# Full-height score matmuls, merged output blocks and a six-slot pipeline in an attention and mixture-of-experts kernel

## The chip, the cores and the metric

The kernel runs on one core of a Trainium2 chip. The metric is the device time of one execution in microseconds (us). "Span" is the time from the first to the last instruction in the trace of one profiled execution.

With one core, a run's state (fast or slow) is known only from its time against the fastest run of the same kernel. Ratios are the mean time of one kernel's fast runs over that of the other's fast runs of the same rounds, so they are not quite the ratio of the medians quoted beside them. A ratio comes with its 95% interval.

In lines of the profile, PE is TensorE's matmuls, PEld its weight loads, DVE VectorE, ACT ScalarE, POOL GpSimd, and L288 is line 288 of the kernel. Brackets hold the idle time before an instruction and what ended it. PSUM is the memory that the matmuls of these kernels write to; copying a result out of it is called evacuating.

## The reference

```python
def attention(q, k, v):              # (4, 8, 768, 64)
    scores = (q @ k.T) / 8
    # heads 0, 2, 6: causal; the other five: causal and (key < 4 or distance < 64)
    a = softmax(masked scores)
    return a @ v

def moe(x, w_skip, w_gate, w1, w2):  # x: (3072, 512), the heads side by side
    todo = (x @ w_skip) > 0          # about half of the tokens
    e = argmax(x @ w_gate); g = softmax(x @ w_gate)[e]       # 8 experts
    out = x
    out[todo] += g * (relu(x @ w1[e]) @ w2[e])               # 512 -> 1024 -> 512
```

Nothing of the second half can start for an expert until every batch has been routed, because a token's place in its expert's list depends on all tokens before it.

## The kernel before

Attention works batch by batch in three passes. `trans` turns Q and K of two heads at a time so that the 64 features lie on the rows of the array. `retr` (causal heads) and `strm` (windowed heads) compute transposed scores, the exponential on ScalarE and a mask. `avx` forms one block of 128 output rows of the batch before, normalizes it, writes it out, casts it, transposes it and computes the gates.

```python
    def trans(b, pr):
        for name, src, dst in (("qT", q_in[b], qT), ("kT", k_in[b], kT)):
            ps = tp.tile([P, NT, P], FP16, tag="t", name="tps")
            for n in range(NT):
                for i, h in enumerate(PAIRS[pr]):          # two heads, 64 rows each
                    nc.tensor.matmul(ps[i * D:(i + 1) * D, n],
                                     src[:, h, n * D:(n + 1) * D], ident, is_transpose=True, ...)
            # ... evacuated alternately by ScalarE and VectorE

    def retr(b, pr, i, c):
        r = slice(i * D, (i + 1) * D)
        # ...
        nc.tensor.matmul(ps[:, o:o + w], kT[b, pr][r, j * P:(j + 1) * P],
                         qT[b, pr][r, q0:q0 + w], start=True, stop=True)

    def avx(b, i):
        for t in range(2):
            o = ap_.tile([P, 4, V1], FP32, tag=f"av{t}", name=f"av{t}")
            # ... output matmuls of four heads, then reciprocal and multiply on VectorE
        # ... DMA of the block
        nc.gpsimd.tensor_copy(x16, xf)                     # cast on GpSimd
        for s in range(DS):
            nc.tensor.matmul(ps[:, s], x16[:, s * P:(s + 1) * P], ident, is_transpose=True, ...)
        nc.scalar.copy(xT, ps)
        # ... gates, at once

    for b in range(B + 1):
        steps = list(front(b)) if b < B else []
        if b < B:
            prep_v(b)                  # copies of V on GpSimd, at the start of the batch
        for i in range(NT):
            if b:
                avx(b - 1, i)
            for f in steps[i * len(steps) // NT:(i + 1) * len(steps) // NT]:
                f()
        if b:
            route(b - 1)
        if b + 2 < B:
            load_qk(b + 2, False)
            load_v(b + 2)
        if b + 1 < NW and b < B:       # NW = 5 experts are loaded in attention
            load_w(b + 1)
```

The experts follow. Sixteen indirect DMAs gather the tokens of eight experts by 128-row tiles, the loads of the other three experts' weights are mixed in among them, and then come two matmul passes and a scatter for each expert.

```python
        for e in range(3):
            gather(e)
        load_w(NW)                     # takes the buffer of the first expert
        for e in range(3, E):
            gather(e)
        for e in range(NW + 1, E):
            load_w(e)
```

The softmax here doesn't subtract the row's maximum and nothing guards it: scores larger than these inputs give would overflow.

## Time and profile before

| | us |
|---|---|
| time, median of the runs beside the changed kernel | 287.84 (286.45 to 289.05) |
| the profiled execution: time, span | 276.55, 274.6 |
| to the last block's gates (attention) | 188.5 |
| from there to the first expert matmul | 14.2 |
| experts | 61.6 |
| end | 10.3 |

The profiled execution was some 10 us faster than every timed one.

One more page row is worth reading. The row of the granted clock (the share of TensorE's full speed, in tenths), in 40 slices of the span:

```profile
PEclk9999999999999999955555555555559999999995
```

It shows nines (full speed) up to about 117 us. The first record of the clock lies at 106.1 us, where a fast stretch of 10.2 us begins. Ahead of this record the row showed full speed while score matmuls of 512 columns took 604 ns (40 to 60 us), against 387 in the fast stretch, so for that part only durations tell. The prediction shows them, with the stages and the waits.

### The profile page before, as it was taken

Reading aid. Unit: us, or ns where it says so; the run is one execution under the profiler, and the core shown is the slowest. Engines: PE = TensorE matmul, PEld = TensorE weight load, DVE = VectorE, ACT = ScalarE, POOL = GpSimd, SP = SyncE. Lnnn points to the kernel's source line nnn. Section 1 sums busy time; section 2 is a strip of 40 time slices with the busy share of each in tenths; the row PEclk is TensorE's granted clock in tenths of the full one; section 3 lists DMA queues with packets and bytes.
Section 4 is the critical chain, followed back from the end, with each engine's and each line's share of the span. In section 5 each row is a group of like instructions: output and inputs, shape, how many; then the busy total and the mean of one; then the engine's idle time right before and its main releaser. Section 6 shows DMA issues by size and latency. Waiting matters only on the chain. (4 is left out here: it accounts for less than half of the span.)

```text
span 274.6 us, 5032 instructions
## 1 busy us (share of the span) xinstructions
PE 207.7 (76%) x1996; PEld 130.6 (48%) x1996; DVE 120.9 (44%) x398; ACT 96.2 (35%) x138; POOL 121.4 (44%) x182
## 2 busy tenths in 40 slices
PE   1797038999838059999599999992179999999940
PEld 0454014655524046665355665661147666666620
DVE  5337104434418125657744357546334454554330
ACT  2568101273822007774055464121033323232200
POOL 8869399525123364281610110110477718325240
PEclk9999999999999999955555555555559999999995
DMA  5997999999999999999020010220276999998110
GB/s 70 164 114 72 191 175 223 247 216 225 227 209 180 216 154 195 235 207 105 24 84 11 38 41 35 83 79 38 66 204 193 160 262 218 211 260 217 42 62 7
DMA packets 53457, 39.52 MB, mean 144 GB/s; under 512 B 28265, under 2 KB 44649, under 8 KB 53424
## 3 DMA queue, kind: packets, MB, share of 16 engines
q0 software_dynamic: 49968, 32.82, 80.2%
q10 hardware_dynamic: 1728, 3.15, 3.2%
q1 hardware_dynamic: 1728, 3.15, 3.2%
q8 instruction: 17, 0.28, 0.4%
q14 instruction: 16, 0.13, 0.2%
HBM read 56.66 MB, written 10.49 MB: 245 GB/s over the span
## 5 line engine op out<-in xcount | busy, mean ns | idle before, releaser
L295 ACT ACTIVATE atr<-sps 128x1024 f16<-128x1024 f32 (+1 forms) x36 | 32.4, 919 | 14.8 <-PE sps L288 14.5
L382 POOL CAST x<-x 128x512 f16<-128x512 f32 x24 | 15.0, 629 | 45.4 <-DVE x L377 26.3
L388 ACT COPY xT<-tps 128x512 f16<-128x512 f16 x24 | 14.1, 587 | 56.4 <-PE tps L385 46.0
L574 PE MATMUL mhp<-mxT,w1t 128*128 128x256 f16 x256 | 30.4, 279 | 0.9
L376 DVE RECIPROCAL rec<-av 128x4 f32<-128x4 f32 x48 | 8.6, 181 | 49.9 <-PE av L366 34.0
L589 PE MATMUL myp<-w2t,ht 128*128 128x512 f16 x128 | 29.9, 379 | 0.0
L366 PE MATMUL av<-va,atr 128*128 128x65 f16 x252 | 23.4, 236 | 7.5 <-POOL va L242 7.5
L574 PEld LDWEIGHTS <-w1t 128*128 128x128 f16 x256 | 25.7, 100 | 7.0 <-issue 2.8
L288 PE MATMUL sps<-qT,kT 64*128 64x512 f16 (+3 forms) x96 | 28.6, 450 | 0.1
L593 POOL DMA_INDIRECT out_dram<-xg,idx x16 | 16.2, 1011 | 26.4 <-DVE xg L591 9.3
L385 PE MATMUL tps<-ident,x 128*128 128x128 f16 x96 | 14.4, 295 | 16.5 <-POOL x L382 16.5
L107 POOL DMA_DIRECT2D va<-in_v_dram x24 | 21.2, 948 | 11.4 <-DMA w2t<-in_moe_w_dram 5.3
L366 PEld LDWEIGHTS <-atr 128*128 128x128 f16 x252 | 15.0, 120 | 15.5 <-issue 13.5
L542 POOL DMA_INDIRECT xg<-out_dram,idg x16 | 16.5, 1030 | 12.8 <-DVE idx L529 8.2
L265 DVE COPY qT<-tps 128x768 f16<-128x768 f16 x16 | 15.3, 958 | 14.6 <-PE tps L255 13.1
L578 DVE TENSOR_SCALAR ht<-mhp 128x512 f16<-128x512 f32 x16 | 11.1, 691 | 23.9 <-PE mhp L574 23.9
L371 PE MATMUL av<-vs,ats 128*64 128x65 f16 x120 | 18.6, 247 | 3.7 <-POOL vs L248 2.0
L377 DVE TENSOR_TENSOR x<-av,rec 128x256 f32<-128x256 f32 x48 | 20.1, 422 | 2.2 <-POOL x L382 0.4
L357 PE MATMUL av<-vsk,esk 20*128 20x260 f16 x48 | 18.1, 383 | 2.3 <-ACT esk L348 1.2
L567 ACT COPY mxT<-mtp 128x512 f16<-128x512 f16 x16 | 8.7, 588 | 31.6 <-PE mtp L565 21.3
L255 PE MATMUL tps<-ident,qin 128*64 128x128 f16 x192 | 14.0, 302 | 6.9 <-DMA qin<-in_q_dram 6.5
L263 ACT COPY kT<-tps 128x768 f16<-128x768 f16 x16 | 12.8, 800 | 18.0 <-PE tps L255 18.0
(130 smaller groups left out, 375.8 us busy)
## 6 DMA issues: line engine op xcount, KB each, us to landing
w1t<-in_moe_w_dram POOLq DMA_DIRECT2D x8, 1024.0 KB, 14.1
w2t<-in_moe_w_dram POOLq DMA_DIRECT2D x8, 1024.0 KB, 17.7
va<-in_v_dram POOLq DMA_DIRECT2D x24, 128.0 KB, 10.3
out_dram<-x ACTq DMA_DIRECT2D x12, 256.0 KB, 4.7
out_dram<-x SPq DMA_DIRECT2D x12, 256.0 KB, 3.7
qin<-in_q_dram POOLq DMA_DIRECT2D x3, 768.0 KB, 15.3
kin<-in_k_dram POOLq DMA_DIRECT2D x3, 768.0 KB, 14.2
qin<-in_q_dram POOLq DMA_DIRECT2D x4, 96.0 KB, 3.8
```

The source lines that it names most:

```text
L107: nc.gpsimd.dma_start(out=va[b][:, i, :, :D], in_=vr[b, i])
L265: nc.vector.tensor_copy(o, i_)
L288: mms = [lambda j=j, q0=q0, o=o, w=w: nc.tensor.matmul(ps[:, o:o + w], kT[b, pr][r, j * P:(j + 1) * P], qT[b, pr][r, q0:q0 + w], start=Tru ...
L295: nc.scalar.activation(a[:, o:o + w], ps[:, :w], ACT.Exp, scale=SCALE)
L357: nc.tensor.matmul(o, esk[b % 2][:, i * P:(i + 1) * P], vsk[:, b, t], start=True, stop=False)
L366: nc.tensor.matmul(o[:, c], a[:, x0:x0 + P], va[b][:, j, h], start=False, stop=fin and j == i)
L371: nc.tensor.matmul(o[:D, c], a[:, q0:q0 + D], vs[b][:, i, u], start=False, stop=fin)
L377: nc.vector.tensor_tensor(x[:, :, t], o[:, :, :D], rec.unsqueeze(2).to_broadcast([P, 4, D]), op=ALU.mult)
L542: nc.gpsimd.indirect_dma_start(out=xg[e, t], out_offset=None, in_=out[:, :], in_offset=bass.IndirectOffsetOnAxis(ap=idg[:, sl:sl + 1], axi ...
L574: nc.tensor.matmul(hp[:, u], w1t[:, s, f * P:(f + 1) * P], xT[:, s], start=(s == 0 and u == 0), stop=(s == DS - 1 and u == 1))
L589: nc.tensor.matmul(yp, hts[e][:, f, t * P:(t + 1) * P], w2t[:, f], start=(f == 0), stop=(f == FS - 1))
L593: sc = nc.gpsimd.indirect_dma_start(out=out[:, :], out_offset=bass.IndirectOffsetOnAxis(ap=idx[:, sl:sl + 1], axis=0), in_=xg[e, t], in_of ...
```

## The change

Its intent: let TensorE's clock be released (raised to full speed) earlier by work that uses the whole array, an idea that experiments 2 and 4 test, and let no engine wait for another inside a batch.

```diff
-NW = 5
+NW = 4
+    kz = {h: [ac.tile([P, S], FP16, name=f"kz{h}_{i}") for i in range(2)] for h in RETR}
+    # the other 64 rows of each are set to zero once, by VectorE
...
-            ps[:, o:o + w], kT[b, pr][r, j * P:(j + 1) * P],
-            qT[b, pr][r, q0:q0 + w], start=True, stop=True)
+            nc.tensor.matmul(ps[:, o:o + w], kz[h][b % 2][:, j * P:(j + 1) * P],
+                             qT[b, pr][:, q0:q0 + w], start=True, stop=True)
...
+    def fills(n):                       # ten matmuls of 512 columns before the first Q has landed
+            nc.tensor.matmul(ps[:, :512], ident, fill, start=True, stop=True)
...
-            rec = tiny.tile([P, 4], FP32, tag=f"rec{t}", name="rec")          # twice a block
+        rec = tiny.tile([P, 2, 4], FP32, tag="rec", name="rec")               # once
...
+        eng = nc.gpsimd if pool else nc.vector          # three window masks in five go to GpSimd
...
-        if b:
-            route(b - 1)                                  # in one go, at the end of a batch
+    for g in range(-NT, G + 2):                           # six slots per batch
+        for f in s0: f()                                  # scores, first half of the slot
+        gates(g - 2)
+        outp(g)
+        for f in s1: f()                                  # scores and transposes, second half
+        flush()                                           # the masks of the slot
+        xt(g - 1)
+        next(routing, None)                               # one of four pieces of the routing
...
-        for e in range(3):
+        for e in range(2):
             gather(e)
-        load_w(NW)
-        for e in range(3, E):
+        load_w(NW, wp2)                 # a pool of its own, in memory that attention gives back
+        for e in range(2, 5):
             gather(e)
-        for e in range(NW + 1, E):
-            load_w(e)
+        load_w(NW + 1, wp2)
+        for e in range(5, E):
+            gather(e)
+        for e in range(NW + 2, E):
+            load_w(e, wp2)
```

The cuts leave out that the score matmuls of two heads are no longer interleaved, fixed tiles for V whose ones and zeros are set once, V being asked for one batch later and ahead of the next Q and K, copies of V in the middle of a batch, the transposes of an expert's tokens two experts ahead, and one comparison for six in the routing.

## The prediction

> **What bounds the kernel now.** I read first the sums by stage, in the stretches that the block starts in the trace mark off: front of batch 0, output blocks of batches 0 to 3, last routing and first gathers, experts, end. The columns are the stretch, its length, then busy us (and instructions) of PE, PEld, DVE, ACT, POOL, the granted clock, the DMA share and GB/s.

> ```profile
> 0.00:35.00 35.00, 18.90 (x187) 11.19 (x188) 14.91 (x42) 16.13 (x20) 26.41 (x48) 1.00 1.25 123
> 35.00:63.20 28.20, 22.51 (x222) 13.20 (x221) 9.01 (x29) 7.96 (x11) 18.54 (x33) 1.00 1.39 216
> 63.20:116.30 53.10, 37.30 (x446) 22.86 (x445) 22.52 (x86) 22.55 (x32) 19.18 (x33) 1.00 1.31 204
> 116.30:158.10 41.80, 38.10 (x390) 22.91 (x388) 22.48 (x79) 20.03 (x29) 14.57 (x24) 0.50 0.56 80
> 158.10:188.50 30.40, 26.97 (x297) 17.35 (x295) 17.04 (x75) 11.03 (x17) 4.82 (x9) 0.50 0.16 62
> 188.50:202.70 14.20, 3.22 (x26) 2.09 (x27) 6.80 (x40) 1.50 (x4) 6.14 (x6) 0.50 0.30 84
> 202.70:264.30 61.60, 60.73 (x437) 40.98 (x436) 26.97 (x45) 17.04 (x30) 30.55 (x31) 0.98 0.86 186
> 264.30:274.60 10.30, 0.00 (x0) 0.00 (x0) 1.11 (x5) 0.00 (x0) 1.21 (x2) 0.61 0.12 38
> ```

> Attention takes 188.5 us of the 274.6, the experts 61.6 with PE busy throughout. In attention no engine but PE is busy over about half of a middle batch (41.8 us: DVE 22.5, ACT 20.0), and PE waits or runs slowly.

> Which of the two, the forms of the score matmul show. The clock column says 1.00 up to 106 us, but it has no record there; the durations decide. First the stretch 40 to 60 us, then 106.1 to 113 us.

> ```profile
> L288 PE MATMUL sps<-qT,kT 64*128 64x512 f16 x4 | 1.8, 604 | 0.0
> ...
> L288 PE MATMUL sps<-qT,kT 64*128 64x512 f16 x4 | 1.5, 387 | 0.0
> ```

> The same form takes 604 ns in one and 387 in the other. At 138 to 158 us it is 605 again. So attention runs on the slow clock from the start, apart from 106.1 to 116.3 us, and the experts (128x512 at 379 ns) on the fast one.[...]

> The third view is the waits, for the stalls; columns: total us, times, longest.

> ```profile
> PE tps L385 <- POOL x L382: 16.5, 5, 9.2
> ...
> PE av L366 <- POOL va L242: 7.5, 1, 7.5
> ...
> POOL va L107 <- DMA w2t<-in_moe_w_dram: 5.3, 1, 5.3
> ```

> PE waits 16.5 us for the cast of an output block on GpSimd. The timeline shows why: GpSimd stands in a DMA issue or behind a tile of V.

> ```profile
> 93.94 0.32 POOL L242 MEMSET va<- 128x48 f16 x1 [5.20 <-DMA va<-in_v_dram]
> ```

> Until that memset and the four copies behind it were done (98.6 us), the cast could not start, and PE stood still from 90.1 to 99.3 us. PE stands still in the same way at 27.9 to 35.4 and 74.9 to 79.7 us.

> [...]PE was busy for 3.41 of 3.41 us in several windows at the slow clock, so instruction busyness isn't what is counted. If I weigh each matmul's columns by the share of rows and columns of the array it uses, the window that released the clock (102.7 to 106.1) had 3,190 full-array columns, the greatest among the slow ones (next 2,960); the fast window before the fallback had 2,680. I take about 3,050 per window as the level: an inference from one release, not a fact. [...]six 64-row score matmuls of two heads take 1.03 us together, as three of one head do.[...]

> **The change part by part.**

> Full-height scores. Keys of heads 0, 2, 6 lie in 128-row tiles whose other half is zero. Columns per head: 1024+1024+640 = 2,688, three heads 8,064 per batch. Heads 0 and 2 no longer run side by side, nor does head 6 beside a windowed head: per batch 2,688 columns added for the first and some 2,200 for the second (three windowed heads of 768, the last beside only 640), 4,900 columns, 4.1 us slow or 2.0 us fast. In exchange these matmuls count whole: full-array columns of a batch rise from about 22,700 to 26,700 (transposes 6,144, scores 8,064, windowed 1,920, sinks 300, output 6,500, transposes of x 3,072, rest 700). Against 3,050 per 3.41 us, a batch has to last less than about 30 us to keep the clock. Before, a middle batch lasted 42.

> Fast clock. All columns of a batch that pass after one another, in the new form: transposes 6,144 (pairs side by side), scores 8,064, windowed 3,840, sinks 1,920, output 9,200, x 3,072, gates and routing about 2,900; sum 35,100.[...]

> Six slots per batch. Transposing x comes one slot after its block, gates two slots after, routing in four pieces. This takes the wait for the cast (16.5 us) off PE, and also most of PE's waits for routing. The other engines per batch: ACT nine exponentials at 0.92, five at 0.81, sinks 0.7, six copies of x at 0.59, four evacuations at 0.80: 19.8 us. DVE: nine triangle masks 2.6, two of five window masks 1.1 (three go to GpSimd), key evacuations now in six pieces, of which the half-height ones have as many columns and so also cost 0.96: 5.8, merged normalization, estimated 0.95 a block from 2 x 0.42 + 2 x 0.18 less one fixed cost, 5.7, routing about 5.5: 20.7. By slot, the larger of the engines is about 4.5 (ACT), 4.2, 5.1, 3.5 (DVE), 2.7 (PE) and 3.2 us, 23.2 in all; slot 2, say, has on DVE two triangles 0.6, a window mask 0.56, one evacuation 0.96, a normalization 0.95 and a routing piece of about 2.1. With a fifth for bubbles: 28 us a batch (estimate). It lies just under the 30 that keep the clock, so I expect the clock to flip: fast in slots 0 to 2 and 5, doubtful in 3 and 4, which have only 2,700 full-array columns (slot 3: scores 640, a windowed head 384, output 1,190, x 512).

> V and ones. The memsets inside the batches go (0.3 us each), the tiles of V are fixed, V of the next batch is asked for before its Q, K and the weights. One expert less is loaded in attention.

> Fillers. Ten matmuls of 512 columns, 4.3 us at the slow clock, in a time when PE waits for the first Q anyway (4.46 us): free, worth at most 2 to 3 us of faster transposes while DMA is the limit.

> Sum, against the stages above:
> - Front of batch 0: the loads still set it. K of batch 1 lands about 34 us, and the copies of V come after GpSimd's issues: 37 us (35.4 before).
> - Three batches with front and output: 3 x 28 = 84. The six blocks of the last batch, without other work and with one output buffer: 6 x 3.2 = 19 (before 2.4 to 4.1 us each). Two slots of drain: 4. Together 107 (153.1 before).
> - Last routing and gathers: 14.2; one comparison for six saves 1, two more gathers before the first matmul cost 1.3: 14.5.
> - Experts: 61.6, with fewer stalls but a fourth expert's weights to load here: 62.6.
> - End: 10.3.
> Sum 231.4 us of span, 43.2 less. The timed median is 13.2 us over the profiled span; I keep that: 244.6, rounded 245.

> **Rivals.** (a) The clock stays slow in most slots, because the level is higher than I think or the windows straddle slots 3 and 4. Then PE needs 29 us plus bubbles, some 34 a batch: 18 us more, 263. For it: PE was "busy" at the slow clock for nearly all of 140 to 170 us. (b) The clock stays fast throughout and slots run at engine limits: 25 a batch, 236; with the DMA-free front a little earlier, 230. For it: once fast, windows of 3,340 and 4,510 held it. (c) GpSimd becomes the wait: three window masks per batch at perhaps 1.3 us (a guess: no such row exists yet), copies of V 3.7, casts 3.8 and some ten issues of 0.9 make 20 us[...]. One slot of slack hides about 4 us; a block of 9 us per batch would cost 5 a batch, 15 in all: 260. (d) The experts wait for weights: four experts of 4.2 MB and 7 MB of gathers and scatters at the 0.43 MB per us that I estimate from the same stage before (20 MB in 47 us) need 56 us, and the last is due about 57 us in. Up to 5 us more.

> **Range and chances.** (a), (c) and (d) add, (b) takes away: 228 to 268 us holds 8 in 10. To miss 2% (282 us) nearly all of the 43 us would have to be lost, which needs (a) and (c) and a longer front: faster 0.94, within 2% 0.04, slower 0.02.

> **What would show it.** Right: 128x512 score matmuls near 385 ns in most of attention; middle batches of 25 to 30 us; no wait of a transpose of x on a cast; experts about 62 us. Wrong: 605 ns there, or records at 0.5 through whole batches (a); long GpSimd gaps ended by DMA or casts that come late (c); PE gaps before the fifth to eighth expert's matmuls that end with a weight DMA (d); a last batch of outputs well over 19 us, as the single output buffer makes every block wait for its normalization.

The stages (37 + 84 + 19 + 4 + 14.5 + 62.6 + 10.3) came to 231.4 us of span, and with 13.2 us over the span to 244.6. Cut is the step that put a batch's 35,100 columns at 29 us on the slow clock and 15 on the fast one, which rival (a) uses. The trace of the kernel before gives about the same, as an estimate: its 64-row score matmuls of 384 and 128 columns took 524 and 311 ns on the slow clock (40 to 100 us) and 323 and 216 on the fast one (106.2 to 116 us), so 0.83 and 0.42 ns per column. The 4.1 and 2.0 us for 4,900 columns agree with that.

What else the text leans on can be read in the same trace. The clock's records change at 106.08, 116.32, 205.07 and 266.51 us, 3, 26 and 18 times 3.41 us apart; these are the windows that the text weighs. An exponential took 692 ns on 20 rows and 706 on 128 for the same 640 columns, which fits the full price put on half-height evacuations (956 ns in the changed kernel, where full height had taken 958). The "fixed cost" in the merged normalization is the author's estimate; the merged multiply and reciprocal measured 692 and 207 ns, so 0.90 us against its 0.95. GpSimd spent 0.76 to 1.02 us on a DMA issue of a whole tile of V, Q, K or weights, and waited up to 5.3 us ahead of one; why it waits was not shown.

## The result, and the profile after

| | before | after |
|---|---|---|
| median, us | 287.84 | 264.6 (260.92 to 267.83) |
| ratio of the fast runs | | 0.9151 [0.9046, 0.9256] |
| profiled execution: span, us | 274.6 | 259.1 |

The output agrees with the reference. The medians differ by 23.2 us, the profiled spans by 15.5: the profiled execution of the kernel before was unusually fast, that of the changed kernel was the fastest of its own runs by 3.7 us.

The changed kernel by stage: front of batch 0; output blocks of batches 0, 1, 2 with the scores of the batch after; output blocks of batch 3; last routing and gathers; experts; end. Columns as in the prediction's table of stages.

```profile
0.00:40.50 40.50, 22.95 (x246) 12.87 (x246) 20.38 (x54) 18.22 (x24) 31.38 (x54) 0.81 1.40 141
40.50:73.90 33.40, 28.80 (x350) 17.45 (x349) 15.43 (x29) 16.86 (x23) 22.67 (x28) 0.67 1.20 213
73.90:109.60 35.70, 30.94 (x392) 20.29 (x390) 19.48 (x56) 19.18 (x27) 23.82 (x31) 0.67 1.32 204
109.60:138.70 29.10, 26.45 (x359) 17.19 (x358) 18.34 (x53) 17.14 (x25) 15.75 (x21) 0.73 0.64 82
138.70:162.00 23.30, 18.33 (x205) 11.95 (x204) 9.90 (x38) 4.34 (x8) 6.48 (x11) 0.50 0.24 73
162.00:186.70 24.70, 2.42 (x26) 1.93 (x27) 7.07 (x36) 1.32 (x3) 10.59 (x11) 0.50 1.15 247
186.70:247.50 60.80, 60.01 (x438) 40.99 (x436) 26.83 (x43) 16.95 (x30) 24.76 (x26) 0.98 0.63 145
247.50:259.10 11.60, 0.00 (x0) 0.00 (x0) 1.17 (x5) 0.00 (x0) 1.29 (x2) 0.61 0.10 34
```

Against the stages before: front +5.1 us, the four output batches 121.5 against 153.1 (31.6 less), routing and first gathers +10.5, experts -0.8, end +1.3. The sum is -15.5, the difference of the spans. So the pipeline won about 32 us in the middle, and half of that was given back at two ends: where attention starts, and where the experts start. (The stages begin with the first output matmul. Counted from the first normalized block, 42.8 us before and 45.7 after, the front lost 2.9 us and the middle won 29.4.)

The score matmuls, first in 117 to 130 us, then in 87 to 116 us:

```profile
L317 PE MATMUL sps<-qT,kz 128*128 128x512 f16 x3 | 1.2, 389 | 0.0
...
L317 PE MATMUL sps<-qT,kz 128*128 128x512 f16 x6 | 3.7, 612 | 1.2 <-DVE kz L268 1.0 <-ACT atr L320 0.2
```

A matmul on 128 rows cost here (389 and 612 ns) what one on 64 rows did (387 and 604 ns). What changed is how long the array is at full speed. From the clock's records, that is 11.1 to 24.7, 48.6 to 55.5, 69.1 to 86.2 and 116.9 to 130.6 us, 51.2 us of attention; before it was one stretch of 10.2. This was the fastest execution; the profile of another (268.69 us, experiment 8) has 44.4 us. Of the 92.5 us between the first normalized block of batch 0 (45.7) and the last of batch 2 (138.2), 37.6 are fast, 41%.

The waits that answer to those of before (total us, times, longest):

```profile
PEld L409 <- ACT xT L404: 10.3, 12, 1.0
...
PE av L409 <- ACT xT L404: 5.7, 9, 0.7
...
PE tps L401 <- POOL x L395: 0.3, 1, 0.3
```

The 16.5 us of waiting for the cast have become 0.3. The gates (L409) now wait for the copy of the transposed block, a microsecond at most at a time, 5.7 us in all for the matmuls. Over the four output batches TensorE's idle time fell from 28.2 to 17.0 us and its busy time from 124.9 to 104.5 (length less busy time, and busy time, of the stage tables).

Then the start of the experts. GpSimd, from the end of attention on (start, us, instruction, idle time before it and what ended it):

```profile
158.85 0.83 POOL L108 DMA_DIRECT2D w1t<-in_moe_w_dram  x1 [2.47 <-PE av L385]
...
160.28 0.89 POOL L110 DMA_DIRECT2D w2t<-in_moe_w_dram  x1
161.16 0.76 POOL L108 DMA_DIRECT2D w1t<-in_moe_w_dram  x1
161.90 0.91 POOL L110 DMA_DIRECT2D w2t<-in_moe_w_dram  x1
168.08 1.13 POOL L581 DMA_INDIRECT xg<-out_dram,idg  x1 [5.27 <-DVE idf L563]
```

And VectorE's first cast of gathered tokens, in the changed kernel and then in the one before:

```profile
184.25 0.86 DVE L603 CAST mx<-xg 128x512 f16<-128x512 f32 x2 [16.06 <-DMA xg<-out_dram,idg]
```

```profile
198.39 0.43 DVE L562 CAST mx<-xg 128x512 f16<-128x512 f32 x1 [4.12 <-DMA xg<-out_dram,idg]
```

The source asks for two experts' tokens first, but GpSimd's instructions stand in another order in the built kernel: the loads of the fifth and sixth expert need only the memory that the last output matmul gives back, and go out at 158.85 to 161.9 us, ahead of the first gather at 168.08. The gather's data came 16 us after its issue; before, 4 us. The volume fits: 24.7 us at 247 GB/s are 6.1 MB, and four weight tiles of 1,024 KB (4.2 MB) with seven gathers of 128 x 512 x 4 bytes (1.8 MB) are 6.0. Before, the sixth expert's tiles had to wait for the buffer of the first, so they did not get ahead of the first gathers (the first of them went out at 211.71 us, behind 13 gathers).

### The profile page after: what moved, and what is told of

Its sections match the earlier page's. It is cut to its first block, busy times and chain, and to the rows that moved or that the text cites. A ratio compares the mean times of both kernels' runs of the same rounds, so it can differ in the third digit from the quotient of the medians.

```text
span 259.1 us, 4963 instructions
## 1 busy us (share of the span) xinstructions
PE 189.9 (73%) x2006; PEld 122.7 (47%) x2006; DVE 118.6 (46%) x313; ACT 94.0 (36%) x138; POOL 136.7 (53%) x178
## 5 line engine op out<-in xcount | busy, mean ns | idle before, releaser
L317 PE MATMUL sps<-qT,kz 128*128 128x512 f16 (+3 forms) x96 | 23.8, 363 | 3.9 <-ACT atr L320 1.7
L581 POOL DMA_INDIRECT xg<-out_dram,idg x16 | 16.5, 1031 | 15.9 <-DVE idf L563 5.3
L345 POOL TENSOR_TENSOR ats<-ats,smask 128x768 f16<-128x768 f16 x12 | 19.8, 1659 | 8.9 <-ACT ats L343 8.8
L388 DVE RECIPROCAL rec<-av 128x8 f32<-128x8 f32 x24 | 5.0, 207 | 40.8 <-PE av L385 40.7
L625 ACT ACTIVATE ht<-mhp 128x512 f16<-128x512 f32 x16 | 9.4, 597 | 33.8 <-issue 20.8
L266 ACT COPY qT<-tps 128x768 f16<-128x768 f16 x16 | 12.8, 800 | 22.5 <-PE tps L276 16.2
L268 DVE COPY kz<-tps 64x768 f16<-64x768 f16 x12 | 11.5, 956 | 20.4 <-PE tps L276 20.0
L606 PE MATMUL mtp<-ident,mx 128*128 128x128 f16 x64 | 6.2, 240 | 18.5 <-issue 18.4
L343 ACT ACTIVATE ats<-sps 128x768 f16<-128x768 f32 x20 | 15.8, 813 | 8.2 <-PE sps L341 8.0
L634 PEld LDWEIGHTS <-ht 128*128 128x128 f16 x128 | 12.3, 98 | 13.5
L636 DVE SCALAR_TENSOR_TENSOR xg<-myp,gs,xg 128x512 f32<-128x512 f32 x16 | 12.0, 750 | 14.1 <-PE myp L634 13.2
L276 PE MATMUL tps<-ident,qin 128*64 128x128 f16 x192 | 13.2, 267 | 7.1 <-DMA qin<-in_q_dram 4.4
```

The source lines that it names most:

```text
L317: nc.tensor.matmul(ps[:, o:o + w], kz[h][b % 2][:, j * P:(j + 1) * P], qT[b, pr][:, q0:q0 + w], start=True, stop=True)
L343: nc.scalar.activation(a, ps[:, :S], ACT.Exp, scale=SCALE)
L345: late.append(lambda: eng.tensor_tensor(a, a, smask.rearrange("p i c -> p (i c)"), op=ALU.mult))
L581: nc.gpsimd.indirect_dma_start(out=xg[e, t], out_offset=None, in_=out[:, :], in_offset=bass.IndirectOffsetOnAxis(ap=idg[:, sl:sl + 1], axi ...
L634: nc.tensor.matmul(yp, hts[e][:, f, t * P:(t + 1) * P], w2t[:, f], start=(f == 0), stop=(f == FS - 1))
```

## The experiments

The main theory was that attention lost 18 us against the prediction because the clock stayed slow for 59% of the middle batches, and that the clock follows something other than the share of the array's rows and columns taken together; and that 10 us more were lost to gathers behind weights. The rivals: waits between engines set the pace of the slots, whatever the clock (W); GpSimd and the landing of V do (called V in experiment 9, G in experiment 7); the fillers do, or cost something.

Each on one chip with the kernel before beside it: the first four kernels below, the next four, and the last four. Medians of different calls are not compared where a ratio can be. But the base of the ratios shifts too: of the executions of the kernel before, 6 of 7, 3 of 9 and 6 of 11 count as fast in the three calls, and the record files every run of the second and third call as "unclear". A difference of 1 or 2% between runs of different calls is therefore not sure.

### 1. Is the gathers' place in the queue the cause?

```diff
+        if tie is not None:
+            nc.gpsimd.tensor_copy(w1t[:, 0, :1], tie)   # the load has to wait for the gathers' index
         nc.gpsimd.dma_start(out=w1t, in_=w1r[e])
...
-        load_w(NW, wp2)
+        load_w(NW, wp2, idg[:, :1])
```

(The same for the other tile, and for the sixth expert.)

> The changed kernel, with one element of the weight tiles of experts 4 and 5 written on GpSimd from the routing result, so that these four loads are issued behind the first gathers and no longer before them. Theory Q (the first gathers lay 16 us in the DMA queue behind four weight transfers of 2 MB): the first expert matmul comes about 8 us after the first gather is issued, as in the kernel before, not 18.6 us; about 10 us less, near 254 us. Rival D (the experts are bound by the loading of their weights, so later loads give it back): the start gains 10 us, PE then waits before experts 4 to 7, and the time stays within 3 us of the changed kernel's 264.6.

Measured: 260.71 us (259.24 to 263.4), ratio 0.8973 [0.8886, 0.9060]. From the first gather's issue to the first expert matmul 7.5 us instead of 18.6. VectorE's first cast, and one some 20 us later:

```profile
177.13 0.43 DVE L607 CAST mx<-xg 128x512 f16<-128x512 f32 x1 [4.40 <-DMA xg<-out_dram,idg]
...
196.37 0.43 DVE L607 CAST mx<-xg 128x512 f16<-128x512 f32 x1 [6.34 <-DMA xg<-out_dram,idg]
```

The first wait fell from 16 to 4.4 us, so the queue's order was its cause. But the expert stage grew from 60.8 to 69.8 us: later gathers now stood behind the weights, and TensorE waited 6.47 us for the second of these casts. Of 11 us won at the start about 9 were given back in that trace (of the execution of 263.4 us). With only two experts' tokens ahead of the weights, the order moved a wait more than it removed one. The median is 3.9 us below the changed kernel's, not 10: rival D held for the larger part.

### 2. Do the rows count? The same columns on 64 rows

```diff
-            nc.tensor.matmul(ps[:, o:o + w], kz[h][b % 2][:, j * P:(j + 1) * P],
-                             qT[b, pr][:, q0:q0 + w], start=True, stop=True)
+            r = slice(i * D, (i + 1) * D)
+            nc.tensor.matmul(ps[:, o:o + w], kz[h][b % 2][r, j * P:(j + 1) * P],
+                             qT[b, pr][r, q0:q0 + w], start=True, stop=True)
```

> The changed kernel with the score matmuls of heads 0, 2 and 6 on their own 64 rows again, in the same order and with the same columns; nothing else differs. Theory R (the clock is released by the share of array rows in use over a window of 3.41 us, 0.75 or more, and kept above about 0.40): the fast share of 41 to 139 us falls from 38% to under 20% and the time rises by 4 to 10 us. Rival U (any busy matmul counts, or the rows are not what matters): fast share and time stay within 1%.

(The 3.41 us, 0.75 and 0.40 of theory R are estimates from the traces of the two kernels; experiment 4 gives the windows.)

Measured: 272.46 us (271.24 to 275.99), ratio 0.9436 [0.9327, 0.9544]. The changed kernel without fillers (experiment 3) ran at 266.11 and 0.9158; the intervals don't touch. The instructions of TensorE and of the other engines are the same; only the rows of the score matmuls differ. Fast time in attention is 20.5 us here, 34.1 in the profile of experiment 3 and 51.2 in the changed kernel's. So the rows are worth some 6 us here (272.46 - 266.11), with the clock as the difference that the traces show. That is about a quarter of the gain (290.49 - 266.11 = 24.4). The rest was won with the clock slow nearly throughout attention, so it comes from the other parts of the change.

### 3. The fillers

```diff
-    fills(10)
```

> The changed kernel without the ten filler matmuls. Theory L (the front of batch 0 waits for loads and GpSimd's issues until about 41 us, whatever the clock): the clock stays slow to beyond 17 us, but the time stays within 1%. Rival F (the fast clock from 11 to 25 us moves the whole front): 3 us or more slower.

Measured: 266.11 us (264.54 to 268.62), ratio 0.9158 [0.9074, 0.9242] against 0.9151 with them. They are worth nothing that these runs can see: in both traces TensorE then waits for Q until about 28.5 us and for K until about 32.7. Two readings were off. The fillers did not run while TensorE waited for the first Q: both kernels wait for the identity matrix until 5.91 us, and with the fillers the transposes began at 10.29 instead of 5.91. And the clock was fast from 13.3 to 23.6 us without them too, where theory L had it slow to beyond 17. So this run says what the fillers are worth, not what a front at the slow clock would cost.

### 4. What the clock follows, by itself

A kernel that computes nothing of use: streams of 512-column matmuls in different shapes, some with about 10 us of rest between them. It writes zeros, so its result is wrong.

```python
    part("pA", [(0, 128, 128)], 40, True)      # (first row, rows, columns of weights), how many, rest after
    part("pB", [(0, 64, 128)], 40, True)
    part("pC", [(0, 128, 32)], 40, True)
    part("pD", [(0, 64, 128), (64, 64, 128)], 40, True)
    part("pE", [(0, 96, 128)], 40, True)
    part("pF", [(0, 128, 128)], 40, False)
    part("pG", [(0, 64, 128)], 60, False)      # no rest: from the fast clock on
    part("pH", [(0, 32, 128)], 60, True)
```

> Not the computation (zeros are written): trains of 512-column matmuls, each after about 10 us of PE rest: pA 128 rows x 128 columns of the array, pB 64 x 128, pC 128 x 32, pD pairs of 64 x 128 side by side, pE 96 x 128; then without rest pF 128 x 128, pG 64 x 128, pH 32 x 128. Theory R (row share): pA, pC, pD and pF become fast after one to two windows, pB stays slow, pE at 0.75 is on the edge, pG (0.5) stays fast, pH (0.25) falls to slow within two windows. Theory C (rows times columns, which the prediction assumed): pC stays slow. Theory U (any busy matmul): pB becomes fast and pH stays fast.

Measured, in stretches of 3.4 us well into pA, pB, pC, pD, pE, pG and pH; the column after the five engines is the granted clock:

```profile
10.00:13.40 3.40, 3.40 (x17) 1.57 (x16) 0.00 (x0) 0.00 (x0) 0.00 (x0) 1.00 1.05 372
37.30:40.70 3.40, 3.40 (x9) 1.18 (x8) 0.00 (x0) 0.00 (x0) 0.00 (x0) 0.50 0.00 0
57.80:61.20 3.40, 3.40 (x18) 1.48 (x17) 0.00 (x0) 0.00 (x0) 0.00 (x0) 1.00 0.03 5
81.70:85.10 3.40, 3.40 (x34) 2.01 (x32) 0.00 (x0) 0.00 (x0) 0.00 (x0) 1.00 0.00 0
102.20:105.60 3.40, 3.40 (x17) 1.52 (x16) 0.00 (x0) 0.00 (x0) 0.00 (x0) 1.00 0.02 5
136.30:139.70 3.40, 3.40 (x17) 1.49 (x16) 0.00 (x0) 0.00 (x0) 0.00 (x0) 1.00 0.00 0
146.50:149.90 3.40, 3.40 (x9) 1.17 (x8) 0.00 (x0) 0.00 (x0) 0.00 (x0) 0.51 0.00 0
```

TensorE was busy for 3.40 of 3.40 us in every line, and the number of matmuls is 9 at the slow clock and 17 or 18 at the fast one (34 for the pairs). A stream on 64 rows left the clock slow (0.50) for its whole length, 17 us. In a stream on 128 rows but only 32 columns of weights, a quarter of the cells, the clock was at 1.00. So it was on 96 rows, and with two 64-row streams side by side. Behind a fast stream, one on 64 rows kept the clock at 1.00 (pG), and one on 32 rows had 0.51 (pH).

### 5. Is the clock what sets the slots? Fillers inside the slots, on 128 and on 64 rows

```diff
+    def hold(n):      # 252 columns of zeros, added to an unused stretch of the output's PSUM tile
+        for i in range(n):
+            nc.tensor.matmul(av[:, 0, 260:512], ident[:128], fill[:128, :252],
+                             start=False, stop=False, skip_group_check=True)
...
+        nh = 0 if g < 0 else 5 if b == B or g >= G else 4 if i > 2 else 0
+        hold(nh)      # ahead of the gates
...
+        hold(nh)      # behind the output block
```

The second kernel has `ident[:64]` and `fill[:64]` in place of 128.

> The changed kernel with more fillers: matmuls of 128 rows and 252 columns into unused PSUM columns, eight in each of slots 3, 4 and 5 of a batch with front and ten in each slot of the last batch, in halves before the gate matmuls and after the output block. Theory R (row share over a window, kept above about 0.40) with the clock as a bound: the fast share of 46 to 160 us, 33% in the changed kernel, rises above 60%, and what the fast clock is worth there (the half-height run lost 8 us with 22 us less of it in its profile) exceeds the fillers' own 0.8 to 1.7 us a slot: 3 to 12 us faster than the changed kernel. Rival W (waits between engines set the slots[...]): the clock is held but the time is the same or longer.

> The same fillers on 64 rows, as many and as long. Theory R: they count half, so the clock is fast for clearly less of the time than with 128 rows, and the time lies 3 us or more above that run. Rival U (any busy matmul counts): no difference between the two beyond 1%.

Measured: on 128 rows 266.94 us (265.48 to 269.02), ratio 0.9328 [0.9204, 0.9452]; on 64 rows 289.63 (288.18 to 290.95), 1.0154 [1.0073, 1.0236]. The sums over 46 to 160 us, in order: the changed kernel, half height (experiment 2), fillers on 128 rows, fillers on 64 rows.

```profile
46.00:160.00 114.00, 98.51 (x1249) 63.81 (x1247) 60.32 (x170) 54.46 (x78) 61.24 (x81) 0.66 0.91 152
```

```profile
46.00:160.00 114.00, 102.99 (x1161) 63.94 (x1157) 58.69 (x165) 53.91 (x76) 59.66 (x78) 0.54 0.92 149
```

```profile
46.00:160.00 114.00, 97.73 (x1287) 65.46 (x1284) 61.70 (x164) 53.16 (x76) 59.42 (x78) 0.82 0.88 148
```

```profile
46.00:160.00 114.00, 105.69 (x1184) 65.93 (x1183) 54.08 (x135) 51.53 (x72) 58.15 (x75) 0.65 0.88 142
```

Two things follow. First, the same 152 fillers cost 22.7 us more on half the rows, with a granted clock of 0.65 against 0.82. 152 x 252 columns are 32 us at the slow pace of pB, 40 matmuls of 512 columns in 17.2 us (estimate), and the time rose by 25 over the changed kernel's 264.6: TensorE was busy for 105.69 of 114 us at that clock of 0.65, so there it was the bound, and what was added to it showed for the larger part. Second, and against the theory: with a clock of 0.82 instead of 0.66 the kernel was no faster than the changed one. Its second batch, from the last block of batch 0 to that of batch 1, ran fast from 72.4 to 96.3 and 99.7 us on and took 31.6 us, against 34.0. The fillers themselves waited:

```profile
L257 PE MATMUL av<-fill,ident 128*128 128x252 f16 x117 | 20.8, 325 | 5.2 <-DVE x L395 5.2
```

They stood behind the normalization of the block, 5.2 us in all, since both use the same PSUM tile. So rival W is right for a part: with the clock fast for 28.2 of its 31.6 us, a batch still took 31.6, and the 24 fillers in it are only 2.6 us of that (estimate from pG, 60 matmuls of 512 columns in 13.1 us). Which wait sets the slot then, one between the kernel's own engines or the fillers' own, these runs do not separate. The fillers bought clock (0.82 for 0.66) with TensorE time (20.8 us for 117 of them), and the median was no lower for it (266.94 against 264.6 us). (The expectation's "22 us less" is a slip: over 46 to 160 us the clock of 0.66 and 0.54 means some 27 us.)

### 6. The fifth expert loaded in attention again, and more gathers ahead of the weights

```diff
-NW = 4
+NW = 5        # room made with single keys tiles, fewer small buffers, no tile for the fillers
-    fills(10)
...
-        for e in range(2):
+        for e in range(5):
             gather(e)
         load_w(NW, wp2, idg[:, :1])
-        for e in range(2, 5):
-            gather(e)
-        load_w(NW + 1, wp2, idg[:, :1])
         for e in range(5, E):
             gather(e)
```

(Against experiment 1, and with the tie of it.)

> The changed kernel with the fifth expert's weights loaded during attention again (single buffers for the padded keys and for some small tiles make the room; the start fillers are gone), ten gathers before the first weight load of the expert stage, which is tied to the routing result. Theory Q+D (the first gathers lay behind weight transfers, and gathers and weights together fill the DMA in the expert stage): gather to first expert matmul about 8 us (18.6), experts about 62 us (60.8; 69.8 with the gathers first and four experts to load), 8 to 11 us less than the changed kernel, near 254 us or a ratio of 0.88 to the kernel before. Rival S (the smaller buffers cost as much in attention): attention to the last block over 164 us, and no gain.

Measured: 257.25 us (255.66 to 258.61), ratio 0.8994 [0.8866, 0.9122], where 264 to 267 us are the changed kernel's. The start of the experts took 8.1 us and their stage 61.5, so the wait was removed this time, not moved. The gain is 3 us short of the expected 254. Part of rival S held: the last block was normalized at 166.6 us, later than the 164 it named (159.6 and 164.1 in two traces of the changed kernel). The second batch shows no clear price in this trace (36.0 us; in those two 34.0 and 36.6), but it does in the traces of the two later versions with five experts (42.8 and 40.9).

### 7. The window masks back on VectorE

```diff
-        eng = nc.gpsimd if pool else nc.vector
+        eng = nc.vector
```

> The changed kernel with all five window masks of a batch on VectorE (0.56 us each before) instead of three on GpSimd (1.66 us each in its profile). Theory N (GpSimd's masks lie in its idle time; casts wait little): within 1%. Rival G (the prediction's rival c: GpSimd's load delays casts and copies of V): 3 us or more faster.

Measured: 260.33 us (258.34 to 263.22), ratio 0.9147 [0.9003, 0.9291]; by the ratio no difference from the changed kernel (0.9151 and 0.9271), by the medians 4 us less than its 264.6 and 264.3. The base decides between the two, so theory N and rival G stay open. The trace shows a local difference. GpSimd's row for the masks in the changed kernel, and two lines of its timeline there:

```profile
L345 POOL TENSOR_TENSOR ats<-ats,smask 128x768 f16<-128x768 f16 x12 | 19.8, 1659 | 8.9 <-ACT ats L343 8.8
```

```profile
35.00 1.64 POOL L345 TENSOR_TENSOR ats<-ats,smask 128x768 f16<-128x768 f16 x1
36.58 1.48 POOL L259 COPY vs<-va 64x1560 f16<-64x1560 f16 x1
```

And the same copy of V with the masks on VectorE:

```profile
34.46 1.49 POOL L259 COPY vs<-va 64x1560 f16<-64x1560 f16 x1
```

A mask took 1,659 ns on GpSimd; on VectorE it took 558 in the kernel before. Of the eight masks that the changed kernel left on VectorE, five took 543 to 559 ns and three 966 to 1,461, each of the three while GpSimd had a mask of its own in work. The cause was not tested. In batch 0 a mask on GpSimd stands ahead of V's copies, which the first output block needs: with the masks on VectorE that block was normalized at 42.3 us instead of 45.7.

### 8. The changed kernel again, and the parts put together

The third call ran the changed kernel once more beside two versions: experiment 6 with the masks of experiment 7, and that with four fillers of 252 columns in slots 3 to 5 of the middle batches.

```diff
+        hold(0 if g < 0 or i < 3 or b == B else 4)     # ahead of the gates alone
```

> The changed kernel itself, for a base on the same chip as the three beside it: 260 to 268 us, ratio 0.90 to 0.93.

> five_early with all window masks on VectorE: the start of the experts after the gathers stays at about 8 us, and if the 260.3 us of the run with the masks on VectorE was a gain and not the spread, 252 to 255 us; if it was the spread, 257 us as five_early.

> five_masks with four fillers of 128 rows and 252 columns ahead of the gates in slots 3, 4 and 5 of a batch with front alone, none behind the output block, where those of the run with many fillers waited for the normalization. If holding the clock pays once the fillers stand where PE waits anyway: 2 to 6 us below five_masks. If other waits set the slots at the fast clock: the same within 1%, or slower.

| | median (range), us | ratio to the kernel before |
|---|---|---|
| the changed kernel again | 264.31 (262.56 to 268.69) | 0.9271 [0.9185, 0.9356] |
| fifth expert and masks | 254.30 (254.01 to 255.05) | 0.8940 [0.8884, 0.8996] |
| the same with a few fillers | 252.72 (249.47 to 254.48) | 0.8809 [0.8722, 0.8897] |

The changed kernel's time repeats within 0.3 us on another chip; its ratio is higher because the kernel before ran at 286.11 there. The fifth expert and the masks together came to 254.30 us, inside the 252 to 255 that would make the masks a gain; but the 257.25 to compare with is of another chip, and the ratios' intervals overlap. The last version is the fastest of all. Its fillers do what the light dose should: the clock was fast for 71.7 us of attention, against 51.2 in the version without them. The gain over the version without is 1.6 us in the medians, the intervals overlap a little, and only three of its six executions count as fast, so it is likely, not sure.

### 9. The new handling of V in the old kernel

```diff
-        if b < B:
-            prep_v(b)
...
+            if i == 4 and b < B:
+                prep_v(b)          # copies of V late in the batch
...
+        if b and b + 1 < B:
+            load_v(b + 1)          # asked for ahead of Q, K and weights
```

(With the fixed tiles of V as well.)

> The kernel before with one part of the change alone: fixed V tiles whose ones and zeros are set at the start, V asked for one batch later and ahead of Q, K and weights, its copies in step 4 of the batch; score matmuls, output blocks and routing as before. Theory V (PE's long stalls of 7.5, 4.8 and 9.2 us came from GpSimd standing at V's tiles and issues): 8 to 20 us faster than the kernel before, ratio 0.93 to 0.97, and no PE gap over 3 us between 45 and 185 us. Rival P (the pipeline of blocks, transposes and routing is what counts): within 2%.

Measured: 281.31 us (278.47 to 284.12), ratio 0.9852 [0.9752, 0.9951]. That lies within the 2% of rival P: theory V fails, and the handling of V explains little of the gain by itself. The stall stays, now before the copies of V:

```profile
89.26 1.48 POOL L246 COPY vs<-va 64x1560 f16<-64x1560 f16 x1 [5.28 <-DMA va<-in_v_dram]
```

TensorE stood still for 9 us behind it, as before. The version with a fifth expert and a few fillers has it too:

```profile
91.70 1.48 POOL L265 COPY vs<-va 64x1560 f16<-64x1560 f16 x1 [10.72 <-DMA va<-in_v_dram]
```

The two traces of the changed kernel, with four experts loaded, have no such wait over 2 us. This suggests that `NW = 4` is an exchange: some 2 MB less in the queue in attention, where V is due, and the same 2 MB ahead of the gathers later. It isn't shown: no run changes `NW` alone, experiment 6 with five experts has no such wait, and the fillers on 128 rows with four have one of 8.2 us.

## Why the prediction was right or wrong

The range (228 to 268) held; the point, 245, was 19.6 us too low. By its own terms:

| term | predicted | measured | off by |
|---|---|---|---|
| front of batch 0 | 37 | 40.5 | +3.5 |
| three batches with front and output | 84 | 98.2 | +14.2 |
| last output batch and drain | 23 | 23.3 | +0.3 |
| last routing and gathers | 14.5 | 24.7 | +10.2 |
| experts | 62.6 | 60.8 | -1.8 |
| end | 10.3 | 11.6 | +1.3 |
| span | 231.4 | 259.1 | +27.7 |
| time over span | 13.2 | 5.5 (264.6 - 259.1) | -7.7 |

**Right: what the pipeline removes.** The wait for the cast went (16.5 to 0.3 us), output-only slots took what was said, the experts didn't wait for a fourth load (rival d), and score matmuls cost the same on twice the rows (389 and 612 ns against 387 and 604). In experiment 2 full height was worth some 6 us, with 34.1 us of fast clock against 20.5, which was the intent of the change and of the prediction's second part.

**Mis-sized: the batch, "28 us a batch".** It measured 32.7 (98.2 / 3). The step that failed is "I expect the clock to flip: fast in slots 0 to 2 and 5". It was fast for 41% of the middle, not for four slots in six. Behind it stands "full-array columns", rows times columns against a level of 3,050: in the probe the rows decided (a clock of 1.00 on 128 rows by 32 columns of weights, 0.50 on 64 by 128). What the prediction called an inference from one release was one, and the wrong one: the window from 65.7 to 69.1 us released the clock with 0.38 by the prediction's count and 0.78 by rows. The batch of 32.7 us lies nearer to rival (a) (slow, 34) than to the main line (28). The other half of this term is that even with the clock fast nearly throughout (one batch of experiment 5) it took 31.6 us, so the sum of slot maxima plus a fifth for bubbles was too low as well.

**Mis-sized: "14.5" for routing and gathers, which failed outright.** I took the order of gathers and loads from the source and counted two more gathers as 1.3 us. The built order had four weight loads ahead, and the first gather's data came 16 us after its issue, not 4. No rival named it: (d) asked whether weights come late for the experts, not whether they make the tokens late. Experiments 1 and 6 show the cause and its cure.

**Mis-sized: the front, 37.** A mask of 1,659 ns on GpSimd (the guess was 1.3 us) stands ahead of V's copies (experiment 7), and held back the first block: 45.7 us, against 42.3 with the masks on VectorE. V's loads of batch 0 also went out later (13.85 us instead of 7.45, behind the sinks' and the gates' small loads), but the copies waited for no DMA there. The fillers, called free, cost nothing and bought nothing, though not for the reason given: they delayed the transposes by 4.4 us, and later waits for Q and K hid it (experiment 3). Rival (c), GpSimd as the wait, was right in kind: blocks were normalized up to 5 us before their cast, for example at 76.8 and cast at 81.9 us, while GpSimd stood in the issues of V and weights from 72.86 to 81.9. One slot of slack hid this from TensorE.

**Wrong in the other direction: "13.2 us over the profiled span; I keep that".** Time over span is 1.7 to 2 us in each execution. The rest was the distance of one lucky profiled execution from the median. It cancelled 7.7 of the 27.7 us missed (27.7 - 7.7 = 20.0, the miss of 19.6 within rounding). So it is partly luck that the range held: with about 2 us in place of 13.2, point and range would have stood some 11 us lower, and 264.6 above the range. Why that execution was faster by 10 us than all timed ones stays open for the larger part. Other executions of the same kernel lie between 282 and 292 us, and a fast stretch in attention goes with some 5 us: in the third call the three with a mean granted clock of 0.82 to 0.84 (0.824 in the profiled one) took 282.3 to 284.0 us, the other eight 285.3 to 290.8.

What also stays open: how the 32 us won in the middle split between the merged normalization, the delayed transposes and the stepped routing, since these can't be undone one by one without rebuilding the loop. Experiments 2 and 9 only size the clock's part (some 6 us) and V's (about 4). The trace of experiment 2 adds this: with the clock fast for only 10 us of the middle, as in the kernel before, the four output batches took 130.5 us, and TensorE was idle for 14.7 of them (before: 153.1 and 28.2). So some 23 of the 32 us came without the clock, 13.5 of them as less waiting of TensorE.

## What to carry to other kernels

Work out what a clock or a queue reacts to with a probe of a few microseconds before building on one trace. Here the clock was 1.00 on 128 rows by 32 columns of weights and 0.50 on 64 by 128, and the same score columns on 64 rows cost some 6 us (experiment 2). So it is worth trying to lay small matmuls across all rows, and to add a few fillers on all rows (1.6 us in the medians of experiment 8, likely, not sure), but not many (266.94 us against 264.6 in experiment 5). When a change gives loads a memory of their own, look at the order in which the engine that issues them will really do it. Here four weight loads that had become free to go early went out at 158.85 to 161.9 us, ahead of the small urgent gathers from 168.08 us on, and the first gather's data came 16 us after its issue. A one-element copy that made the loads depend on the gathers' index brought that to 4.4 us, but the time fell by only 3.9 us while few gathers went out before the loads (experiment 1); with ten ahead, and a fifth expert loaded in attention, the start took 8.1 us and the experts 61.5 (experiment 6). And compare a predicted span with spans: a median less one profiled span may be luck rather than overhead.
